# A 64-byte row instead of an 8-byte row in a routing table that is scattered to DRAM

## The chip, the cores and the metric

The kernel runs on one core of one Trainium2 chip. The metric is the device time of one execution in microseconds (us). The core has a matrix engine (PE, with its weight loads as PEld), a vector engine (DVE), a scalar engine (ACT), a general engine (POOL, GpSimd) and a queue engine (SP). DMAs are issued from SP and from POOL.

## The reference

The kernel computes block-causal attention and then a two-level mixture of experts on its output.

```
q, k, v: [8 batches, 8 heads, 576 positions, 64], float32
scores = q k^T / 8, masked so that block i (64 positions) sees blocks j <= i
x = softmax(scores) v, as 4608 tokens x 512
g      = argmax(x w_group)       over 4 groups, weight from the softmax
e      = argmax(x w_expert[g])   over 4 experts of the group, weight from the softmax
out[t] = (group weight * expert weight) * (relu(x[t] w1[g,e]) w2[g,e])
w1[g,e]: 512 x 1024, w2[g,e]: 1024 x 512, 16 experts in all
```

Each token is sent to one expert of 16. So between the two halves there is a routing step, which groups the tokens by expert.

## The kernel before, in words

**Attention.** Work goes by pairs of heads: 4 pairs in a batch, 32 pairs. One pass of the loop (a period) runs the tokens of a list that is written out by hand (`ORDER`): scores of one pair, row maxima, exponentials, transposes, the products with v, and the preparation of the next pair. The engines' queues keep the order of this list. In a plain period the products with v of one half head pair (`PE o L329`, 20 matmuls) come 11.3 us apart.

**The moves of q and k.** Each pair needs copies of its transposed q and k in the other half of the partitions. POOL makes them: `shift` (line 234, three moves a period, tokens W0 to W2), `dup` (lines 221 to 224) and `pad` (line 230). The score matmuls (`PE s L254`) read what these moves write, so PE waits if POOL is late.

**The router.** When the last pair of a batch is through, the tokens of the batch's router run among those of the next pairs: logits, argmax, and a rank of each token within its expert (`phase0` to `phase4`). Then `scatter` (line 802) writes one row for each token into a table in DRAM, `tab`: 16 experts with 5120 rows each and 640 rows behind them that stand for "no token", 82,560 rows in all. A row holds two 32-bit numbers, the token's number and its weight. The 576 rows of a batch go in five indirect DMAs from POOL, four of 128 rows and one of 64, each behind a tiny memset of `mark`. The rank makes tokens of one expert lie side by side in the table. In the hand-written list the five scatters (tokens Z0 to Z4) stand between the moves W0 and W1 of a period, and the program makes the first move behind them wait until all five have landed. For the first five batches that place is the same; in the sixth batch three scatters stand ahead of the move at line 221 and two between W0 and W1. The scatters of batches seven and eight have no moves of q and k behind them.

**The fill.** Before the first scatter the whole table is filled with "no token". `setup` does this from POOL in the periods 2 to 7 of attention, as a generator that hooks call five times a period.

**The readers.** In the second half, `getids` (line 881) reads an expert's part of the table back into SBUF with DMAs from SP, 37 in all. An indirect DMA from POOL then gathers the tokens' rows of x (line 892), PE transposes them and multiplies them with w1 and w2 (`h`, `y`), and another indirect DMA scatters the rows of the result, 2 KB each, to the output (line 1048). The weights stream in on SP's queue all the while.

Of the kernel before, what the change touches and what calls it, by code (L numbers as in the profile page):

```python
# [11 lines left out]
I32 = mybir.dt.int32  # L12
# [5 lines left out]
P = 128  # L18
# [393 lines left out]
NTB = 5  # L412
# [3 lines left out]
PADS = NE * REG  # L416
TABR = PADS + 640
R = 64
UNIT = 16
FULL = 512 // UNIT  # L420
CAPS = [33, 28, 28, 26, 20, 20, 18, 17, 16, 16, 12, 9, 9, 8]
# [12 lines left out]
class Router:  # L434
# [10 lines left out]
    def setup(self):  # L445
        nc, fixed = self.nc, self.fixed
        w = fixed.tile([P, 4, 64], F32, name="wcat")
        nc.vector.memset(w, 0.0)
        for z in range(2):
            ps, c0 = slice(64 * z, 64 * z + 64), 32 * z  # L450
            yield
            nc.gpsimd.dma_start(w[ps, :, c0:c0 + 4], self.w_group.rearrange("(c p) g -> p c g", p=P)[ps])
            for g in range(4):
                yield
                nc.gpsimd.dma_start(w[ps, :, c0 + 4 + 4 * g:c0 + 8 + 4 * g],
                                  self.w_expert[g].rearrange("(c p) e -> p c e", p=P)[ps])
        self.w = w
        self.lt = fixed.tile([P, 2, NTB * P], F32, name="lt")
        nc.vector.memset(self.lt[:, :, S:], 0.0)
        yield  # L460
        self.desc = fixed.tile([P, NTB, 4], F32, name="desc")
        for j in range(4):
            nc.gpsimd.memset(self.desc[:, :, j], float(4 - j))
        self.ones = fixed.tile([P, P], BF16, name="ones")
        nc.gpsimd.memset(self.ones, 1.0)
        self.tri = fixed.tile([P, P], BF16, name="tri")
        nc.gpsimd.affine_select(out=self.tri, in_=self.ones, pattern=[[1, P]], compare_op=ALU.is_gt,
                                fill=0.0, base=0, channel_multiplier=-1)

        def iota(name, sh, pattern, cm, base=0):  # L470
            t = fixed.tile(sh, F32, name=name)
            nc.gpsimd.iota(t, pattern=pattern, base=base, channel_multiplier=cm,
                           allow_small_or_imprecise_dtypes=True)
            return t

        self.base = iota("base", [P, NE], [[REG, NE]], 0)
        self.eb = iota("eb", [R, NE], [[REG, NE]], 0)
        self.pid = iota("pid", [R, 1], [[0, 1]], 1)
        self.p512 = iota("p512", [R, 1], [[0, 1]], 512)
        self.p128 = iota("p128", [R, 1], [[0, 1]], 128)  # L480
        self.edesc = iota("edesc", [R, NE], [[-1, NE]], 0, NE)
        yield
        self.vals = fixed.tile([R, 3, 2, NE], F32, name="vals")
        nc.gpsimd.iota(self.vals[:, 0], pattern=[[0, 2], [1, NE]], base=0, channel_multiplier=0,
                       allow_small_or_imprecise_dtypes=True)
        nc.gpsimd.memset(self.vals[:, 1], float(FULL))
        self.scan = [fixed.tile([R, 2 * NE], F32, name=f"scan{i}") for i in range(2)]
        for t in self.scan:
            nc.gpsimd.memset(t, 0.0)
        self.onesf = fixed.tile([R, R], F32, name="onesf")  # L490
        nc.gpsimd.memset(self.onesf, 1.0)
        self.trif = fixed.tile([R, 2, R], F32, name="trif")
        for z, op in ((0, ALU.is_ge), (1, ALU.is_gt)):
            nc.gpsimd.affine_select(out=self.trif[:, z, :], in_=self.onesf, pattern=[[1, R]], compare_op=op,
                                    fill=0.0, base=0, channel_multiplier=-1)
        self.pre = [fixed.tile([P, NTB + 1, NE], BF16, name=f"pre{i}") for i in range(2)]
        for t in self.pre:
            nc.vector.memset(t[:, 0, :], 0.0)
        self.mark = fixed.tile([1, 1], F32, name="mark")
        self.taken = fixed.tile([R, NE], F32, name="taken")  # L500
        yield
        fill = fixed.tile([P, 128, 2], I32, name="fill")
        nc.gpsimd.memset(fill[:, :, 0], NTOK)
        nc.gpsimd.memset(fill[:, :, 1], 0)
        for h in range(5):
            nc.gpsimd.dma_start(self.tab[h * 16384:(h + 1) * 16384].rearrange("(p c) t -> p c t", p=P), fill)
            yield
        nc.gpsimd.dma_start(self.tab[PADS:TABR].rearrange("(p c) t -> p c t", p=P), fill[:, 0:(TABR - PADS) // P, :])
        zrow = self.rows.tile([1, 512], F32, tag="row", name="zrow")
        nc.vector.memset(zrow, 0.0)  # L510
        nc.gpsimd.dma_start(self.xd[NTOK:NTOK + 1, :], zrow)
        yield
        self.cap = fixed.tile([R, 1], F32, name="cap")
        nc.gpsimd.memset(self.cap, 0.0)
        for n, c in enumerate(sorted(set(CAPS))):
            nc.gpsimd.affine_select(out=self.cap, in_=self.cap, pattern=[[0, 1]], compare_op=ALU.is_ge, fill=float(c),
                                    base=-sum(1 for x in CAPS if x >= c), channel_multiplier=1)
            if n % 4 == 3:
                yield
        yield  # L520
# [40 lines left out]
    def final(self, row):  # L561
# [4 lines left out]
        ri = self.t(dt=I32)  # L566
        stt(x, UNIT - 1.0, self.taken, ALU.add, ALU.subtract, out=ri)
        fi = ts(ri, 9, ALU.arith_shift_right, dt=I32)
        ci = ts(ri, UNIT.bit_length() - 1, ALU.arith_shift_right, FULL - 1, ALU.bitwise_and, dt=I32)
        cf, ff = self.t(), self.t()  # L570
# [45 lines left out]
    def spill(self, at, row, cnti):  # L616
# [5 lines left out]
        xi = self.t(one, I32)  # L622
        ts(x, 0.0, ALU.max, P // UNIT - 1.0, ALU.add, out=xi)
        xi = ts(xi, (P // UNIT).bit_length() - 1, ALU.arith_shift_right, sh=one, dt=I32)
        ov = self.t(one)
        V.tensor_copy(ov, xi)
        st = stt(self.cap, float(UNIT), self.res[:, 2:3], ALU.mult, ALU.add, sh=one)
        rhs = self.t([R, 4, R])
# [118 lines left out]
    def phase2(self, at, b, st):  # L747
        nc = self.nc
        full = [P, NTB, 4, 4]
        o16 = self.pool.tile(full, BF16, tag="o16", name=f"o16{b}")  # L750
        st["o16"] = o16
        nc.vector.tensor_tensor(
            out=o16, in0=st["goh"].unsqueeze(3).broadcast_to(full),
            in1=st["eoh"].unsqueeze(2).broadcast_to(full), op=ALU.mult)
        nc.vector.memset(o16[64:128, 4], 0.0)
        pre = self.pre[b % 2]
        for z in range(NTB):
            nc.vector.tensor_tensor(out=pre[:, z + 1, :], in0=pre[:, z, :],  # L758
                                    in1=o16[:, z].rearrange("p g e -> p (g e)"), op=ALU.add)
        gs = self.pool.tile([P, NTB], F32, tag="gs", name=f"gs{b}")  # L760
        es = self.pool.tile([P, NTB], F32, tag="es", name=f"es{b}")
        nc.vector.tensor_reduce(out=gs, in_=st["gex"], op=ALU.add, axis=AX.X)
        nc.vector.tensor_reduce(out=es, in_=st["eex"], op=ALU.add, axis=AX.X)
        nc.vector.tensor_scalar_add(es, es, 1e-9)
        nc.vector.scalar_tensor_tensor(out=gs, in0=gs, scalar=1e-9, in1=es, op0=ALU.add, op1=ALU.mult)
        pay = self.pool.tile([P, NTB, 2], I32, tag="pay", name=f"pay{b}")
        st["pay"] = pay
        nc.gpsimd.iota(pay[:, :, 0], pattern=[[P, NTB]], base=b * S, channel_multiplier=1)
        nc.vector.reciprocal(pay[:, :, 1].bitcast(F32), gs)
# [56 lines left out]
class Moe:  # L826
# [41 lines left out]
    def getids(self, s):  # L868
        if "ids" in s:
            return  # L870
        self.index(s)
        nc = self.nc
        s["ids"] = ids = self.ip.tile([P, 5, 2], I32, tag="ids", name=f"ids{s['n']}")
        table = lambda o, n: self.ro.tab[bass.ds(s["st"] + o, n), :]
        full = s["T"] // P
        todo = [(ids[:, 0:full, :], table(0, full * P).rearrange("(c p) t -> p c t", p=P))] if full else []
        r = s["T"] % P
        if r:
            todo += [(ids[z:z + r, full, :], table(full * P, r)) for z in ((0, s["gap"]) if s["tail"] else (0,))]
        for o, i in todo:  # L880
            self.ro.after_writes(nc.sync.dma_start(o, i))
# [313 lines left out]
def attention_moe(ctx, tc, q, k, v, w_group, w_expert, w1, w2, out, order=None, on_dve=None):  # L1195
    nc = tc.nc
# [2 lines left out]
    NBAT = q.shape[0]  # L1199
    N = 4 * NBAT  # L1200
    dp = ctx.enter_context(tc.tile_pool(name="dp", bufs=1, space=bass.MemoryType.DRAM))
    tab = dp.tile([TABR, 2], I32, name="tab")
    xd = dp.tile([NTOK + 1, 512], F32, name="xd")
    cp = ctx.enter_context(tc.tile_pool(name="cp", bufs=1))
    consts = make_consts(tc, cp)
# [6 lines left out]
    with tc.manual_schedule(engines={ET.PE, ET.Activation, ET.DVE, ET.Pool, ET.SP}):  # L1212
# [34 lines left out]
        b = lambda kk, j: ro.token(at, last, (kk, j))  # L1247
# [62 lines left out]
```

## Time and profile before

| what | value |
|---|---|
| time, median of 3 runs | 932.01 us (930.56 to 936.88) |
| the profiled execution's own time | 927.65 us |
| its span in the profile | 925.9 us |
| busy share of the span: PE, PEld, DVE, ACT, POOL | 93%, 78%, 63%, 56%, 37% |
| mean granted clock of PE | 0.972 |
| attention, up to about | 445 us |
| scatters to the table (line 802) | 40, 994 ns each on POOL, 6.0 us in the middle from issue to landing |
| fills of the table (line 506) | 5 of 128 KB, 2.1 us in the middle from issue to landing |

The profile is of one execution; the times of the runs differ from it by up to 9 us. A line such as `PE s L254 <- POOL qk L234: 31.2, 6, 8.3` in the view of waits says that PE at line 254, which writes `s`, waited for what POOL wrote to `qk` at line 234, for 31.2 us in total, six times, at most 8.3 us. In the view in order of time a row gives the start, the duration, the engine, the line, what is written and read, the count, and in brackets the idle time before it with what ended it. In the chain of waits a DMA's row runs from its issue to its landing. A granted clock of 1.00 is PE's full speed.

### The profile page before, as it was taken

The page shows a single profiled execution, that of the slowest core. Times are in us where ns is not written, and L with a number is a line of the kernel's source. Part 1 is how long each engine was busy: PE and PEld are TensorE (multiplying, and loading weights), DVE is VectorE, ACT ScalarE, POOL GpSimd, SP SyncE. Part 2 cuts the span into 40 slices and gives each one's busy share as a digit, 9 for nine tenths or more (in the row PEclk, how much of TensorE's full clock was granted, in tenths as well). Part 3 has the DMA queues.
Part 4 walks back from the last instruction along what each step waited for, and adds up shares of the span by engine and source line. Part 5 has one row for each costly group of instructions (what it writes and reads, how often), then busy time and mean ns, then how long its engine had stood idle before and what let it go on. Part 6 is the DMA issues. An engine that isn't in the chain of part 4 may idle for free.

```text
span 925.9 us, 16914 instructions
## 1 busy us (share of the span) xinstructions
PE 864.8 (93%) x5649; PEld 723.6 (78%) x5649; DVE 584.3 (63%) x1390; ACT 520.4 (56%) x1374; POOL 343.0 (37%) x555
## 2 busy tenths in 40 slices
PE   7999978989897998969998999999999999999996
PEld 5788857767785876757676887888888888988885
DVE  6778866878787796865873425446354465655562
ACT  6988866868786685856432425344243354645451
POOL 7785435454643545443251312322121123122011
PEclk9999998999999898998998999999999999999999
DMA  5452541526244252515732546555565557655671
GB/s 118 101 121 63 119 88 44 118 46 145 63 107 100 56 114 39 123 34 178 91 104 108 173 141 218 169 175 171 177 203 153 153 193 229 208 186 166 179 240 41
DMA packets 181432, 121.59 MB, mean 131 GB/s; under 512 B 125814, under 2 KB 156534, under 8 KB 181344
## 3 DMA queue, kind: packets, MB, share of 16 engines
q1 hardware_dynamic: 173296, 100.73, 41.4%
q0 software_dynamic: 8048, 19.76, 6.4%
q8 instruction: 46, 0.75, 0.4%
q14 instruction: 42, 0.34, 0.2%
HBM read 100.88 MB, written 19.70 MB: 130 GB/s over the span
## 4 chain that ended last, share of the span: by engine, by line
PE 72%; DVE 9%; DMA 8%; POOL 4%; issue 3%; ACT 3%; SPq 0%; POOLq 0%; DVEq 0%; ACTq 0%
PE h L977 17%; PE y L1022 17%; PE s L254 7%; PE o L329 7%; PE tp L297 6%; DMA tab<-pay,pi 5%; PE y L1027 4%; PE h L972 3%; DVE nm L268 2%; POOL tab L802 2%; PE tp L176 2%; PE ye L1022 2%; PE xp L945 2%; DVE pre L758 2%; DVE qk L200 2%
## 5 line engine op out<-in xcount | busy, mean ns | idle before, releaser
L268 DVE TENSOR_REDUCE nm<-s 128x1 f32<-128x384 f32 (+4 forms) x288 | 142.3, 513 | 81.2 <-PE s L254 79.3
L278 ACT ACTIVATE pb<-s,nm 128x384 f32<-128x384 f32 (+4 forms) x288 | 160.1, 562 | 38.0 <-DVE nm L268 37.2
L254 PE MATMUL s<-qk 128*128 128x256 f32 (+3 forms) x512 | 139.3, 365 | 42.4 <-POOL qk L234 31.2
L977 PE MATMUL h<-xt,wh 128*128 128x264 f32 (+6 forms) x704 | 155.3, 312 | 0.0
L929 DVE TENSOR_TENSOR wl<-raw,wh 128x512 fp32r<-128x512 f32 x192 | 123.5, 684 | 10.6 <-ACT wh L928 10.3
L977 PEld LDWEIGHTS h<-xt,wh 128*128 128x128 f32 x704 | 119.3, 188 | 9.1
L309 ACT COPY pt<-tp 128x512 f32<-128x512 f32 (+1 forms) x224 | 116.9, 548 | 13.8 <-PE tp L297 13.1
L254 PEld LDWEIGHTS s<-qk 128*128 128x128 f32 x512 | 78.5, 197 | 58.8 <-POOL qk L234 32.6
L234 POOL CAST qk<-qk 64x1152 fp32r<-64x1152 f32 x93 | 107.2, 1153 | 34.9 <-DMA tab<-pay,pi 31.9
L297 PE MATMUL tp<-ident,pb 128*128 128x128 f32 x800 | 114.8, 279 | 0.5 <-ACT pt L309 0.4
L1048 POOL DMA_INDIRECT out_dram<-ys,ids x40 | 42.5, 1062 | 187.1 <-DVE ys L1044 175.2
L977 PE MATMUL h<-xt,wl 128*128 128x264 f32 (+6 forms) x352 | 109.3, 311 | 0.0
L928 ACT CAST wh<-raw 128x512 fp32r<-128x512 f32 x192 | 109.1, 620 | 0.2
L1022 PE MATMUL y<-wh,hring 128*128 128x512 f32 x306 | 107.2, 401 | 0.0
L994 DVE SCALAR_TENSOR_TENSOR hring<-h,hring 128x32 fp32r<-128x32 f32 (+7 forms) x112 | 35.7, 356 | 103.1 <-ACT hring L990 99.9
L329 PE MATMUL o<-pt,vb 128*64 128x320 f32 (+4 forms) x896 | 100.5, 364 | 0.1
L297 PEld LDWEIGHTS tp<-ident,pb 128*128 128x128 f32 x800 | 95.1, 144 | 4.9 <-issue 1.2
L990 ACT ACTIVATE hring<-h 128x288 fp32r<-128x288 f32 (+7 forms) x62 | 28.9, 466 | 118.7 <-PE h L977 53.7
L329 PEld LDWEIGHTS o<-pt,vb 128*64 128x64 f32 x896 | 60.1, 137 | 41.2 <-issue 6.4
L892 POOL DMA_INDIRECT xg<-xd,ids x40 | 40.4, 1011 | 104.5 <-DMA ids<-tab 46.5
L221 POOL CAST qk<-qk 64x576 fp32r<-64x576 f32 x31 | 20.6, 665 | 139.5 <-DVE qk L307 121.4
L977 PEld LDWEIGHTS h<-xt,wl 128*128 128x128 f32 x352 | 66.2, 188 | 1.2
(228 smaller groups left out, 1512.3 us busy)
## 6 DMA issues: line engine op xcount, KB each, us to landing
raw<-in_moe_w_dram SPq DMA_DIRECT2D x96, 512.0 KB, 4.1
natk<-in_k_dram SPq DMA_DIRECT2D x32, 256.0 KB, 3.7
natq<-in_q_dram SPq DMA_DIRECT2D x32, 256.0 KB, 4.4
vb<-in_v_dram SPq DMA_DIRECT2D x64, 128.0 KB, 3.1
xd<-xns SPq DMA_DIRECT2D x32, 256.0 KB, 2.6
wh<-in_moe_w_dram SPq DMA_DIRECT2D x16, 512.0 KB, 5.0
rawe<-in_moe_w_dram SPq DMA_DIRECT2D x8, 512.0 KB, 6.8
natk<-in_k_dram SPq DMA_DIRECT2D x32, 32.0 KB, 4.0
```

What stands on the lines that cost most here:

```text
L234: self.nc.gpsimd.tensor_copy(o, s.bitcast(F32))
L254: nc.tensor.matmul(st[:, 0, 0:w], lhsT=r[a][z][:, q0:q0 + P], rhs=r[c][z][:, 0:w], start=x == 0, stop=x == 1)
L268: self.nc.vector.tensor_reduce(out=r["nm"][:, t:t + 1], in_=r["s", t], op=ALU.max, axis=AX.X if t < 8 else AX.XY, negate=True)
L278: nc.scalar.activation(reg, r.pop(("s", t)), AF.Exp, bias=r["nm"][:, t:t + 1], accum_out=self.sms[b][:, pr, t % 2, t // 2:t // 2 + 1])
L297: nc.tensor.transpose(out=o, in_=pb[:, POFF[x] + j * P:POFF[x] + (j + 1) * P], identity=self.c["ident"])
L309: self.nc.scalar.copy(dst, src)
L329: nc.tensor.matmul(o[64 * a:64 * a + 64, BLK * (t - b0):n], lhsT=r["v"][:, a, j, :], rhs=p[:, a], start=x == 0, stop=x == len(pcs) - 1, ti ...
L928: nc.scalar.copy(h[:, sl], s["raw", u][:, sl])
L929: nc.vector.tensor_tensor(out=l[:, sl], in0=s["raw", u][:, sl], in1=h[:, sl].bitcast(F32), op=ALU.subtract)
L977: nc.tensor.matmul(o, lhsT=ww[:, dc, f], rhs=rr[:, dc, t], start=dc == 0 and x == 0, stop=dc == 3 and x == 2)
L1022: nc.tensor.matmul(y[c][0:n], lhsT=hh, rhs=w, start=k == 0 and x == 0, stop=k == 7 and x == 2)
L1048: i = nc.gpsimd.indirect_dma_start(out=self.out, out_offset=bass.IndirectOffsetOnAxis(ap=s["ids"][0:n, c, 0:1], axis=0), in_=ys[0:n], in_o ...
```

## The change

A row of the table becomes 16 numbers of 32 bits (64 bytes), of which the first two are used as before. The table grows from 0.66 to 5.28 MB. Four things follow:

- The fill is a tile of 64 rows of 64 bytes on each partition (4 KB), cleared whole and then given its first column. It goes out in ten DMAs of 512 KB where there were five of 128 KB, two for each call of the generator.
- The payload of the scatter (`pay`) has 16 numbers for each token. It lies in two fixed tiles, which are cleared once beside the fill and used in turn, where it had two buffers of a pool.
- The scatter writes 64 bytes for each token. Its code is the same.
- The readers take the first two numbers of each row, so they still move 8 bytes for each token, now 64 bytes apart.

```diff
+TROW = 16
@@ setup
-        fill = fixed.tile([P, 128, 2], I32, name="fill")
+        fill = fixed.tile([P, 64, TROW], I32, name="fill")
+        nc.gpsimd.memset(fill, 0)
         nc.gpsimd.memset(fill[:, :, 0], NTOK)
-        nc.gpsimd.memset(fill[:, :, 1], 0)
-        for h in range(5):
-            nc.gpsimd.dma_start(self.tab[h * 16384:(h + 1) * 16384].rearrange("(p c) t -> p c t", p=P), fill)
-            yield
+        self.pays = [fixed.tile([P, NTB, TROW], I32, name=f"pay{i}") for i in range(2)]
+        for t in self.pays:
+            nc.gpsimd.memset(t, 0)
+        for h in range(10):
+            nc.gpsimd.dma_start(self.tab[h * 8192:(h + 1) * 8192].rearrange("(p c) t -> p c t", p=P), fill)
+            if h % 2:
+                yield
@@ phase2
-        pay = self.pool.tile([P, NTB, 2], I32, tag="pay", name=f"pay{b}")
+        pay = self.pays[b % 2]
@@ getids
-        table = lambda o, n: self.ro.tab[bass.ds(s["st"] + o, n), :]
+        table = lambda o, n: self.ro.tab[bass.ds(s["st"] + o, n), 0:2]
@@ attention_moe
-    tab = dp.tile([TABR, 2], I32, name="tab")
+    tab = dp.tile([TABR, TROW], I32, name="tab")
```

The order of the instructions is the same on PE, DVE, ACT and SP. It differs on POOL, at the fill. POOL's queue there, before:

```order
L503 MEMSET fill 128x128
L504 MEMSET fill 128x128
L506 DMA tab<-fill 128x256
L230 CAST qk_123<-qk_123 64x576
L223 CAST qk_123<-qk_123 64x512
L224 CAST qk_123<-qk_123 64x64
L506 DMA tab<-fill 128x256 x2
L221 CAST qk_122<-qk_122 64x576
L234 CAST qk_122<-qk_122 64x1152
L506 DMA tab<-fill 128x256 x2
L234 CAST qk_122<-qk_122 64x1152 x2
```

And POOL's queue at the same place in the changed kernel, whose lines behind the fill are numbered up to five higher:

```order
L504 MEMSET fill 128x1024
L505 MEMSET fill 128x64
L508 MEMSET pay_901 128x80
L508 MEMSET pay_902 128x80
L510 DMA tab<-fill 128x1024 x2
L230 CAST qk_123<-qk_123 64x576
L223 CAST qk_123<-qk_123 64x512
L224 CAST qk_123<-qk_123 64x64
L510 DMA tab<-fill 128x1024 x4
L221 CAST qk_122<-qk_122 64x576
L234 CAST qk_122<-qk_122 64x1152
L510 DMA tab<-fill 128x1024 x4
```

Two memsets and one DMA more stand ahead of the moves at lines 230 to 224, and two DMAs more at each of the two places that follow.

At the scatters the order stays. POOL's queue with the semaphores that it waits for, first group of scatters, before:

```order
L802 DMA tab<-pay_1761,pi_1831 82560x2
L801 MEMSET mark 1x1 [waits Pool_49]
L802 DMA tab<-pay_1761,pi_1831 82560x2
L801 MEMSET mark 1x1 [waits Pool_49]
L802 DMA tab<-pay_1761,pi_1831 82560x2
L234 CAST qk_123<-qk_123 64x1152 [waits DMASW3_49,DMASW4_49,DMASW2_49,DMASW5_49,DMASW1_49,DVE_49]
```

The same place in the changed kernel:

```order
L807 DMA tab<-pay_901,pi_1839 82560x16
L806 MEMSET mark 1x1 [waits Pool_49]
L807 DMA tab<-pay_901,pi_1839 82560x16
L806 MEMSET mark 1x1 [waits Pool_49]
L807 DMA tab<-pay_901,pi_1839 82560x16
L234 CAST qk_123<-qk_123 64x1152 [waits DMASW2_49,DMASW6_49,DMASW1_49,DMASW7_49,DMASW0_49,DVE_49]
```

The move at line 234 waits for five DMA semaphores (`DMASW`), one for each scatter, before and after; only their numbers moved, since five more DMAs of the fill took their turns.

## The prediction

> **What bounds the kernel now.** I read the page first, then the view of waits, the chain of waits in order of time, and PE in order of time at the places that these name. By the page PE is busy for 93% of the span, so a gain has to come from the places where PE stands still or runs slowly. Of PE's waits one is much longer than the others, and POOL's queue shows its cause:
>
> ```profile
> PE s L254 <- POOL qk L234: 31.2, 6, 8.3
> POOL qk L234 <- DMA tab<-pay,pi: 31.9, 6, 8.9
> ```
>
> PE's scores wait for POOL's moves of q and k, and those wait for the scatters to the table. The chain of waits has seven scatters in it (start, us from issue to landing), each the last that a move waits for:
>
> ```profile
> 130.40 9.71 DMA tab<-pay,pi
> ...
> 189.73 4.42 DMA tab<-pay,pi
> ...
> 242.54 3.96 DMA tab<-pay,pi
> ...
> 293.63 7.70 DMA tab<-pay,pi
> ...
> 350.68 5.78 DMA tab<-pay,pi
> ...
> 398.95 6.63 DMA tab<-pay,pi
> ...
> 409.24 4.99 DMA tab<-pay,pi
> ```
>
> PE in order of time shows six stalls, one for each of the first six batches (idle time in brackets):
>
> ```profile
> 141.46 1.22 PE L254 MATMUL s<-qk 128*128 128x512 f32 x2 [8.34 <-POOL qk L234]
> ```
> ```profile
> 195.64 1.22 PE L254 MATMUL s<-qk 128*128 128x512 f32 x2 [3.06 <-POOL qk L234]
> ```
> ```profile
> 247.84 0.74 PE L254 MATMUL s<-qk 128*128 128x512 f32 x2 [2.48 <-POOL qk L234]
> ```
> ```profile
> 302.67 1.22 PE L254 MATMUL s<-qk 128*128 128x512 f32 x2 [6.18 <-POOL qk L234]
> ```
> ```profile
> 357.86 1.22 PE L254 MATMUL s<-qk 128*128 128x512 f32 x2 [4.34 <-POOL qk L234]
> ```
> ```profile
> 415.57 1.22 PE L254 MATMUL s<-qk 128*128 128x512 f32 x2 [6.77 <-POOL qk L234]
> ```
>
> They add up to 31.17 us. In the first five, landing less stall is 1.37, 1.36, 1.48, 1.52 and 1.44 us: a stall is the landing of the last scatter less about 1.4 us, one for one. In the sixth two landings (6.63 and 4.99) stand ahead of one stall. There is a second price. The same two matmuls take 0.74 us behind the shortest stall and 1.22 behind the others. About 4 us behind each stall, with the granted clock as the first number behind the five engines' busy times:
>
> ```profile
> 141.46:145.50 4.04, 4.04 (x16) 3.65 (x17) 1.92 (x5) 2.17 (x7) 2.54 (x4) 0.50 0.02 4
> 195.64:199.70 4.06, 4.06 (x21) 3.67 (x22) 2.17 (x5) 2.21 (x8) 2.54 (x4) 0.64 0.00 0
> 247.84:251.90 4.06, 4.05 (x30) 3.79 (x31) 3.25 (x8) 3.12 (x10) 3.68 (x6) 1.00 0.01 1
> 302.67:306.70 4.03, 4.03 (x16) 3.63 (x17) 1.90 (x5) 2.17 (x7) 2.54 (x4) 0.50 0.00 0
> 357.86:361.90 4.04, 4.04 (x16) 3.65 (x17) 1.92 (x5) 2.17 (x7) 2.54 (x4) 0.50 0.01 2
> 415.57:419.60 4.03, 4.03 (x16) 3.64 (x17) 1.25 (x2) 1.83 (x5) 3.67 (x6) 0.50 0.74 197
> ```
>
> Behind the stall of 2.48 us the clock is full; behind 3.06 it is 0.64, and behind the longer ones 0.50 for 4 us. So a stall of 3 us and more costs another 1.5 to 2 us: length times (1 - clock) gives 2.0 four times and 1.5 once, 9.5 us. A stall of up to 2.5 us costs itself alone. The Trainium skill, "TensorE: Matmul & The Clock Gate", Part 1, says that an idle window of about 3.4 us halves PE's clock until it has been busy that long again; the rows agree, with the step somewhere between 2.48 and 3.06 us here.
>
> **The change, part by part.**
>
> *The scatter writes 64 bytes for a token.* POOL's instruction has the same 128 indices, and I cost it the same, since rows of 2 KB (line 1048) and of 8 bytes (line 802) take nearly the same time to issue:
>
> ```profile
> L1048 POOL DMA_INDIRECT out_dram<-ys,ids x40 | 42.5, 1062 | 187.1 <-DVE ys L1044 175.2
> ```
> ```profile
> L802 POOL DMA_INDIRECT tab<-pay,pi x40 | 39.8, 994 | 28.0 <-DVE pi L796 19.0 <-issue 8.0 <-POOL mark L801 1.0
> ```
>
> The question is the landing. While the fourth group is under way, from 298.7 us to its landing at 301.3 us, the bus is empty:
>
> ```profile
> DMA packets 2, 0.00 MB, mean 0 GB/s; under 512 B 2, under 2 KB 2, under 8 KB 2
> ```
>
> The data are out, and only the word that they have landed is late. So bandwidth isn't what holds the scatter. The nearest operation is the scatter of the result: same queue, same kind of instruction, rows of 2 KB. In the stretch 850 to 921 us its landings are
>
> ```profile
> DMA to landing us min/median/max: 1.9/2.8/4.0
> ```
>
> and in its group of 557 to 564 us, where weights and other transfers are on the bus,
>
> ```profile
> DMA to landing us min/median/max: 4.5/6.0/7.8
> ```
>
> That bounds a 64-byte scatter by 1.9 and 7.8 us; below 1.9 nothing is in sight, since POOL's instruction alone takes 1 us of it. The fourth group, the second longest, had a quiet bus at its end, so I stay near the quiet rows: 3.4 us, the middle between 2.8 (whole rows of 2 KB, quiet) and 4.0 (3.96, the best of the seven with 8-byte rows). Why should it fall at all? Tokens of one expert lie side by side, so eight 8-byte rows share 64 bytes, and 128 writes of one scatter meet in a few such places. That the landing of a DMA of whole rows is short and that of 8-byte rows long with an empty bus is what I would expect if those writes are put through one after another. It is an inference; no row shows it.
>
> With 3.4 us a stall is 2.0 us: five stalls make 10.0, and the sixth 6.77 - (6.63 - 3.4) - (4.99 - 3.4) = 1.95. That removes 31.17 - 11.95 = 19.2 us. All stalls are then under 2.48, so the 9.5 us of slow clock go too. Behind them PE itself is next, which is busy nearly all of a plain period.
>
> *The fill.* The prices of POOL's instructions on the page:
>
> ```profile
> L891 POOL MEMSET xge<- 128x512 f32 x4 | 2.1, 535 | 0.0
> L506 POOL DMA_DIRECT2D tab<-fill x5 | 2.8, 557 | 0.3 <-POOL fill L504 0.3
> ```
>
> and the place in POOL's time:
>
> ```profile
> 59.57 0.23 POOL L503 MEMSET fill<- 128x128 int32 x1
> ...
> 60.84 0.68 POOL L230 CAST qk<-qk 64x576 fp32r<-64x576 f32 x1
> 61.45 0.62 POOL L223 CAST qk<-qk 64x512 fp32r<-64x512 f32 x1
> ```
>
> From the first memset to the move at 230 it is 1.27 us now. After: a memset of 1024 columns, 2 x 0.535 = 1.07; three small ones at 0.23 each, the row at 59.57 (estimate); the 0.3 of wait that stands on the page; two issues, 1.11. That is 3.17 us, 1.9 more. Here PE waits for these moves already:
>
> ```profile
> PEld s L254 <- POOL qk L223: 0.5, 2, 0.3
> ```
>
> So the 1.9 us go through to PE. The other four issues (4 x 0.557 = 2.2 us) and what is carried along fall ahead of moves that PE needs later:
>
> ```profile
> 66.32 2.35 POOL L234 CAST qk<-qk 64x1152 fp32r<-64x1152 f32 x2
> ```
> ```profile
> 71.74 0.73 PE L254 MATMUL s<-qk 128*128 128x512 f32 x2
> ```
>
> The move ends at 68.7 and PE needs it at 71.7, later by its own delay of 1.9: 4.9 us of cover against 4.1, so nothing. Without that cover it would be at most 2.2 us.
>
> *The bytes of the fill.* 5.24 MB on the bus between 60 and about 80 us, beside loads of q, k and v of 0.86 MB a period. Large writes run at
>
> ```profile
> DMA packets 220, 0.39 MB, mean 279 GB/s; under 512 B 29, under 2 KB 29, under 8 KB 220
> ```
>
> (stores of x, 297.2 to 298.6 us). (5.24 + 0.86) / 0.279 = 21.9 us, so all is through at 82 us. The load that is needed first is that of v:
>
> ```profile
> 67.15 0.60 SPq L157 DMA_DIRECT2D vb<-in_v_dram  x1
> ```
> ```profile
> 84.02 0.87 PE L329 MATMUL o<-pt,vb 128*64 128x256 f32 x8
> ```
>
> It is needed at 84.0 + 1.9 = 85.9. Hidden, with 4 us to spare. At the mean of 62.8 to 67 us,
>
> ```profile
> DMA packets 2315, 0.90 MB, mean 214 GB/s; under 512 B 2231, under 2 KB 2231, under 8 KB 2314
> ```
>
> it would end at 88.5 (28.5 us) and cost 2.6 us; that is my upper bound. The first scatter waits for the fill, but only at 125 us.
>
> *The readers* move as many pieces of 8 bytes, from places 64 bytes apart. Their DMAs make POOL wait, and PE waits for the gather behind them once:
>
> ```profile
> POOL xg L892 <- DMA ids<-tab: 46.5, 6, 15.1
> ...
> PE xp L945 <- DMA xg<-xd,ids: 4.3, 1, 4.3
> ```
>
> I take nothing, and 1 us at most if the first load lands later. The two fixed payload tiles take turns as the two buffers did: nothing.
>
> **The sum.** 19.2 + 9.5 - 1.9 = 26.8 us off the profiled execution's own 927.65 us: 900.9. The median of the runs, 932.01, lies 4.4 us above; the same 26.8 off it is 905.2. Landings differ from 3.96 to 9.71 within one execution, and if that luck makes the spread of the runs, it goes with it. I forecast **903 us**. With a landing of 2.8 the stalls are 1.4 (five) and 0.75, 7.75 in all: 23.4 + 9.5 - 1.9 = 31.0, 896.6.
>
> **Rivals.**
>
> *Only the long ones shrink.* The landing falls to 4.2 us, between 3.96 and 4.42, as the two quickest groups have it with 8 bytes. Stalls: 5 x 2.8 and 3.55, 17.6 in all, 13.6 less; of the 9.5 us of clock half, since 2.8 lies between 2.48 and 3.06. 13.6 + 4.8 - 1.9 = 16.5: 911 to 915 us. For it: 3.96 and 4.42 come close to the 2 KB rows' 2.8 to 4.0. Against it: nothing names a cause that would spare them.
>
> *A write of 64 bytes is as slow as one of 8.* What a small write costs isn't the neighbours but that it is small, and 64 bytes are small. The landings stay, and the fill remains: 927.65 + 1.9 = 929.5, by the median 933.9. This is also the case in which the change does nothing of what it does. For it: no row of this trace has a write to DRAM between 8 bytes and 2 KB, apart from the fill's 1 KB, which lands in 2.1 us by the table above. Against it: nothing separates the two readings. The Trainium skill, "DMA: Bandwidth & Descriptors", Specifications, says that below 512 bytes a DMA engine reads, changes and writes back; by that rule 64 bytes would gain nothing over 8.
>
> *Slower: landing goes by the number of places.* If eight neighbours are taken together now, a scatter touches some 16 to 32 places of 64 bytes and then 128. Landings would go to the 2 KB rows' worst, 7.8 us, against a mean of 6.17 now (43.19 / 7). (7.8 - 6.17) x 7 = 11.4 us of stalls, 2.5 of clock (the groups at 2.48 and 3.06 go to half clock for 4 us), 1.9 of fill: 15.8, 943.5 us, by the median 947.8. It decides from a mean landing of about 7 us. Against it: 2 KB rows touch most places and land soonest when the bus is quiet.
>
> **Chances.** Forecast 0.44, the weaker gain 0.22, nothing 0.22, slower 0.12. The range reaches from the landing of 2.8 us (896.6, less a little for the spread: 895) to the case of nothing by the median (934); the slower case is left out. A change of 1% is about what a measurement of this kernel can tell from none, so faster is below 922.7 us: 0.66. Within 1% is the case of nothing: 0.22. Slower: 0.12.
>
> **What would show it.** The wait of the score matmuls for POOL falls from 31.2 to about 12 us; the seven landings are about 3.4; no stretch behind a group has the clock at 0.50; PE loses about 2 us near 64 us to the moves behind the fill. If the landings stay at 4 to 10 us, the inference on 8-byte rows is wrong. If they fall and the time doesn't, something behind PE in the same period was as late, and I have missed it. If PE waits for `vb` or `natk` between 80 and 95 us, the fill's bytes weren't hidden.

## The result, and the profile after

| what | before | after |
|---|---|---|
| time, median (lowest to highest), 4 runs each | 931.28 us (923.77 to 936.88) | 899.12 us (897.42 to 901.33) |
| span of the profiled execution | 925.9 us | 895.7 us |
| mean granted clock of PE | 0.972 | 0.994 |

The ratio is 0.966, with a 95% interval of 0.959 to 0.973. The forecast was 903 us, its range 895 to 934. One run of a later experiment (E7) took 1196.51 us at a granted clock of 0.654 and is left out of its figures.

The view of waits of the changed kernel (us in all, times, longest). PE has no row for POOL's moves at line 234 any more; its longest rows are these:

```profile
PE s L254 <- ACT pb L278: 11.4, 17, 1.3
PE xp L950 <- DMA xg<-xd,ids: 5.0, 1, 5.0
PE xn L678 <- ACT xT L309: 4.9, 5, 1.4
PE o L329 <- ACT lt L309: 2.0, 5, 0.4
```

And of POOL's rows those on the table:

```profile
POOL xg L897 <- DMA ids<-tab: 44.8, 6, 14.3
...
POOL qk L234 <- DMA tab<-pay,pi: 6.6, 5, 1.4
...
POOL qk L221 <- DMA tab<-pay,pi: 2.0, 1, 2.0
```

POOL's wait for the scatters at line 234 went from 31.9 us to 6.6 and PE's wait for POOL there from 31.2 to nothing. The first group of scatters in order of time, with the last scatter at 130.25 us:

```profile
127.54 2.22 PE L329 MATMUL o<-pt,vb 128*64 128x320 f32 x20
...
130.25 0.97 POOL L807 DMA_INDIRECT tab<-pay,pi  x1 [0.22 <-issue]
...
132.61 0.43 ACT L309 COPY xT<-o 128x320 f32<-128x320 f32 x1 [3.14 <-PE xn L678]
132.67 2.35 POOL L234 CAST qk<-qk 64x1152 fp32r<-64x1152 f32 x2 [1.45 <-DMA tab<-pay,pi]
132.72 0.62 DVE L268 TENSOR_REDUCE nm<-s 128x1 f32<-128x256 f32 x2 [3.07 <-PE xn L678]
...
133.09 0.66 PE L678 MATMUL xn<-ident,xT 128*128 128x128 f32 x4 [1.39 <-ACT xT L309]
```

The move behind the last scatter starts 2.42 us after that scatter's start; before it was 9.86 us (130.40 to 140.26). Something else is late now. ACT's copy of `o` needs the 20 matmuls that end at 129.76 us, and starts only at 132.61; DVE is held up as long. Before, the same matmuls ended at 129.94 us and ACT's copy started at 129.99, with 0.34 us of idle time ahead of it. PE then waits for ACT, 1.39 us here. The same stands behind the last scatter of each of the first five batches.

Behind it the clock is full; the same 4 us as the prediction's first stretch, in the same columns:

```profile
134.94:139.00 4.06, 4.06 (x32) 3.80 (x31) 3.26 (x8) 3.74 (x13) 2.63 (x6) 1.00 0.34 127
```

The distance from one start of the 20 matmuls at line 329 to the next gives what a period with scatters takes. Its first one, before and after:

```profile
127.72 2.22 PE L329 MATMUL o<-pt,vb 128*64 128x320 f32 x20
...
151.42 2.27 PE L329 MATMUL o<-pt,vb 128*64 128x320 f32 x20
```
```profile
127.54 2.22 PE L329 MATMUL o<-pt,vb 128*64 128x320 f32 x20
...
142.07 2.28 PE L329 MATMUL o<-pt,vb 128*64 128x320 f32 x20
```

That is 23.70 us and 14.53 us. All periods with scatters, read in this way, in this and the later runs:

| kernel | six periods with scatters, us | sum |
|---|---|---|
| before | 23.70, 16.96, 15.00, 21.16, 19.04, 21.03 | 116.89 |
| after | 14.53, 14.19, 14.67, 14.29, 14.74, 13.52 | 85.94 |
| after, once more (E5) | 13.46, 13.12, 13.15, 13.22, 13.14, 13.78 | 79.87 |
| before, once more (E10) | 20.57, 15.45, 14.84, 19.00, 15.45, 20.78 | 106.09 |
| 64-byte rows, 8 bytes written (E1) | 13.40, 13.15, 13.14, 13.18, 13.12, 13.70 | 79.69 |
| the same, eight neighbours in 64 bytes (E11) | 21.56, 18.87, 16.12, 20.74, 18.76, 21.09 | 117.14 |
| the same, four neighbours in 64 bytes (E12) | 18.22, 13.11, 13.15, 16.03, 14.04, 15.22 | 89.77 |
| rows of 16 bytes (E3) | 14.77, 13.09, 13.13, 16.07, 13.96, 13.28 | 84.30 |
| rows of 32 bytes (E2) | 13.43, 13.13, 13.15, 13.19, 13.16, 13.32 | 79.38 |
| rows of 128 bytes (E8) | 13.42, 13.11, 13.16, 13.19, 13.14, 13.17 | 79.19 |
| 64-byte rows, scatters elsewhere (E4) | 12.46, 12.46, 12.46, 12.45, 12.46, 13.10 | 75.39 |

After against before, that is 30.95 us; the period ahead of the sixth is 0.97 us longer now (14.16 against 13.19), which leaves 29.98. The spans differ by 30.2 us. So the whole gain lies in these periods, and the half behind attention is as long as it was (484.6 us behind the last start of the 20 matmuls, 484.2 before).

The fill in the changed kernel, POOL in order of time:

```profile
59.63 0.96 POOL L504 MEMSET fill<- 128x1024 int32 x1
...
61.21 1.18 POOL L510 DMA_DIRECT2D tab<-fill  x2 [0.20 <-POOL pay L508]
62.38 0.68 POOL L230 CAST qk<-qk 64x576 fp32r<-64x576 f32 x1
```

The move at line 230 starts at 62.38 us, 1.5 later than before (60.84). PE's next round of 20 matmuls isn't later, before and after:

```profile
67.41 2.22 PE L329 MATMUL o<-pt,vb 128*64 128x320 f32 x20
```
```profile
67.50 2.22 PE L329 MATMUL o<-pt,vb 128*64 128x320 f32 x20
```

With the fill's bytes the share of the DMA engines goes from 0.51 to 0.86, but PE's busy time in the stretch stays, 22.93 of 23 us (stretch, length, busy PE, PEld, DVE, ACT, POOL with counts, clock, share of the DMA engines, GB/s), before and after:

```profile
57.00:80.00 23.00, 22.93 (x188) 18.59 (x186) 18.03 (x40) 19.58 (x61) 19.64 (x37) 1.00 0.51 119
```
```profile
57.00:80.00 23.00, 22.93 (x188) 18.61 (x186) 17.52 (x41) 19.80 (x62) 21.55 (x43) 1.00 0.86 287
```

### The profile page after: what moved, and what is told of

It is laid out like the page before. It is cut to its first block, busy times and chain, and to the rows that moved or that the text cites. A ratio compares the mean times of both kernels' runs of the same rounds, so it can differ in the third digit from the quotient of the medians.

```text
span 895.7 us, 16921 instructions
## 1 busy us (share of the span) xinstructions
PE 852.5 (95%) x5649; PEld 710.8 (79%) x5649; DVE 583.8 (65%) x1390; ACT 518.4 (58%) x1374; POOL 348.5 (39%) x562
## 4 chain that ended last, share of the span: by engine, by line
PE 80%; DVE 10%; ACT 4%; DMA 2%; issue 2%; SPq 0%; another core or an unknown queue 0%; POOLq 0%; DVEq 0%; ACTq 0%
PE y L1027 18%; PE h L982 17%; PE s L254 8%; PE o L329 8%; PE tp L297 7%; PE y L1032 4%; PE h L977 4%; DVE nm L268 3%; ACT pb L278 3%; PE tp L176 2%; PE xn L678 2%; PE s L263 2%; PE xp L950 2%; DVE pre L763 2%; DVE qk L200 2%; PE ye L1027 2%
## 5 line engine op out<-in xcount | busy, mean ns | idle before, releaser
L268 DVE TENSOR_REDUCE nm<-s 128x1 f32<-128x384 f32 (+4 forms) x288 | 141.9, 513 | 51.4 <-PE s L254 37.2
L254 PE MATMUL s<-qk 128*128 128x256 f32 (+3 forms) x512 | 134.2, 353 | 14.4 <-ACT pb L278 11.4
L934 DVE TENSOR_TENSOR wl<-raw,wh 128x512 fp32r<-128x512 f32 x192 | 123.5, 684 | 10.6 <-ACT wh L933 10.3
L297 PE MATMUL tp<-ident,pb 128*128 128x128 f32 x800 | 110.6, 273 | 0.5 <-ACT pt L309 0.4
L254 PEld LDWEIGHTS s<-qk 128*128 128x128 f32 x512 | 75.3, 190 | 30.9 <-ACT pb L278 15.4
L297 PEld LDWEIGHTS tp<-ident,pb 128*128 128x128 f32 x800 | 91.1, 140 | 4.3 <-ACT pt L309 0.6
L897 POOL DMA_INDIRECT xg<-xd,ids x40 | 42.1, 1054 | 101.5 <-DMA ids<-tab 44.8
```

Source lines behind the costliest of these rows:

```text
L254: nc.tensor.matmul(st[:, 0, 0:w], lhsT=r[a][z][:, q0:q0 + P], rhs=r[c][z][:, 0:w], start=x == 0, stop=x == 1)
L268: self.nc.vector.tensor_reduce(out=r["nm"][:, t:t + 1], in_=r["s", t], op=ALU.max, axis=AX.X if t < 8 else AX.XY, negate=True)
L297: nc.tensor.transpose(out=o, in_=pb[:, POFF[x] + j * P:POFF[x] + (j + 1) * P], identity=self.c["ident"])
L934: nc.vector.tensor_tensor(out=l[:, sl], in0=s["raw", u][:, sl], in1=h[:, sl].bitcast(F32), op=ALU.subtract)
```

## The experiments

Three questions were open. Why do 8-byte rows land late: because neighbours share 64 bytes, or because the writes are small? Where does the new idle time of ACT and DVE come from? And did the fill cost nothing because it is cheap, or because it is covered? E1 to E10 ran on one chip and E11 and E12 on another; which chip gave the two runs above isn't on record. Runs of the kernel before stood beside them: E1 to E4 with a median of 922.73 us for it, E5 to E10 with 924.74, E11 and E12 with one run of 924.24.

**E1: 64-byte rows, 8 bytes written.**

```diff
-        nc.vector.tensor_copy(pi, pf)
+        nc.vector.tensor_scalar(out=pi, in0=pf, scalar1=float(TROW // 2), scalar2=None, op0=ALU.mult)
...
-            out=self.tab, out_offset=bass.IndirectOffsetOnAxis(ap=st["pi"][0:n, c:c + 1], axis=0),
-            in_=st["pay"][0:n, c, :], in_offset=None)
+            out=self.tab.rearrange("n (z t) -> (n z) t", t=2), out_offset=bass.IndirectOffsetOnAxis(ap=st["pi"][0:n, c:c + 1], axis=0),
+            in_=st["pay"][0:n, c, 0:2], in_offset=None)
```

> The table keeps its 64-byte rows, with fill and readers as in the changed kernel, but a scatter writes only the first 8 bytes of a row: each index is 8 times the row. So the writes are as small as in the kernel before, and no two of them share 64 bytes. Theory A, of the prediction (8-byte neighbours that share 64 bytes are put through one after another): nothing changes against the changed kernel; the move behind the last scatter starts 2.2 to 2.4 us after that scatter's start, POOL's wait for the table at the first shift stays near 6.6 us, time 897 to 902 us. Theory B (a small write is slow because it is small): the move starts 4 to 10 us behind the last scatter, POOL's wait is near 32 us, PE's wait for these moves near 31 us, time 929 to 935 us.

Measured: 889.80 us (889.22 to 891.12), ratio 0.966 (0.960 to 0.973). In the chain of waits the last scatters of the groups land soon, though the writes have 8 bytes:

```profile
130.50 2.11 DMA tab<-pay,pi
...
179.54 2.11 DMA tab<-pay,pi
...
228.56 2.12 DMA tab<-pay,pi
```

The last scatter is the one that counts. An earlier one of a group can land later, 4.85 us behind its issue in the fourth group, and is still through first. PE's wait for the moves is there and small:

```profile
PE s L254 <- POOL qk L234: 3.4, 5, 0.9
```

**E11: the same, with eight neighbours in 64 bytes again.** One number differs from E1:

```diff
-        nc.vector.tensor_scalar(out=pi, in0=pf, scalar1=float(TROW // 2), scalar2=None, op0=ALU.mult)
+        nc.vector.tensor_scalar(out=pi, in0=pf, scalar1=1.0, scalar2=None, op0=ALU.mult)
```

> The kernel in which a scatter writes 8 bytes of each 64-byte row, with one number changed: the index is the row itself and no longer 8 times the row, so that eight neighbours share 64 bytes again. Table, fill, write size and order stay. The readers still read at the old places, so the second half works on wrong rows and few results are written; only attention is to be compared. Theory A (neighbours in 64 bytes wait for one another): the move behind the last scatter starts 3.8 to 8 us after it, as in the kernel before, instead of 2.25; PE's wait for POOL at the scores is 20 to 32 us instead of 3.4; periods with scatters of 14.8 to 21 us instead of 13.2. Theory H (the larger table or its fill made the landings short): 2.25 us and 13.2 us stay.

Measured: 928.08 us in one run, of which the half behind attention, on wrong rows, says nothing. The chain and PE's wait are as in the kernel before:

```profile
131.25 7.97 DMA tab<-pay,pi
...
188.46 5.56 DMA tab<-pay,pi
...
243.19 3.53 DMA tab<-pay,pi
```
```profile
PE s L254 <- POOL qk L234: 28.5, 6, 6.8
```

Table, fill and size of the writes are the same in E1 and E11, and only the places differ. Landings of 2.1 us became 3.5 to 8.0, and the six periods 79.69 became 117.14 us. The two ran on different chips, but E12, on E11's chip and with 2.0 for that number, takes 89.77. So it is how close the neighbours lie in the table, as theory A has it. Theories B and H have fallen. That the writes are put through one after another, A's mechanism, no row shows.

**E2, E3, E12: two and four neighbours.** E2 and E3 are the changed kernel with other row sizes:

```diff
-TROW = 16
+TROW = 8
```

> Rows of 32 bytes, written whole; two tokens of one expert that lie side by side share 64 bytes (eight did in the kernel before). Theory A: at most two writes in a row meet in one place, so the start of the move behind the last scatter is 2.3 to 3 us after it, time 898 to 903 us. Theory B with a bound at 64 bytes: as the kernel before, 4 to 10 us, 929 to 935 us. Theory B with a cost in steps of size: between the two, 3 to 5 us and 905 to 920 us.

```diff
-TROW = 16
+TROW = 4
```

> Rows of 16 bytes, written whole; four neighbours share 64 bytes. Theory A: a quarter to a half of the extra landing of the kernel before (mean 6.17 us against some 2.3): 3 to 4.5 us, PE's wait for the moves 5 to 18 us, time 903 to 918 us. Theory B with a bound at 64 bytes: 929 to 935 us.

E12 is E1 with `scalar1=2.0`:

> The same with the index twice the row: 8 bytes are written every 16 bytes, so four neighbours share 64 bytes and half of the bytes between them are not written. The readers read wrong places here too; only attention is to be compared. Theory A: as with rows of 16 bytes written whole, 2.2 to 3.8 us behind the last scatter, PE's wait for POOL 5 to 10 us, periods of 13.1 to 16 us. If what counts is the bytes that a scatter writes in one place rather than the number of its writes there (32 of 64 bytes as with two rows of 16): 2.25 us everywhere. If 8-byte writes are slow in themselves once any share 64 bytes: 4 us and more.

Measured: E2 891.05 us (889.30 to 891.74), ratio 0.968 (0.961 to 0.974). E3 896.54 us (895.95 to 897.04), ratio 0.973 (0.967 to 0.980). E12 900.83 us in one run. In E12, too, only attention is to be compared. PE's waits for the moves in E3 and in E12:

```profile
PE s L254 <- POOL qk L234: 7.5, 6, 2.3
```
```profile
PE s L254 <- POOL qk L234: 10.3, 6, 4.1
```

Two neighbours in 64 bytes cost nothing that can be seen: E2's periods are those of E1. Four cost in some batches: E3's periods of batches two and three stay at 13.1 us, the fourth is 16.07. Eight cost in all. So the loss begins between a distance of 32 bytes and one of 16. It goes by the distance and not by the bytes written: in E12 four writes put 32 bytes into 64 and cost, in E2 two put 64 there and don't. That 64 bytes is the size of the place that counts isn't shown. Places of 32 bytes, of which each takes one write without loss, fit these rows as well, and so does a loss that grows with how densely the writes lie. Why 8 bytes with gaps cost more than 16 whole bytes in the first and the sixth period (18.22 and 15.22 us against 14.77 and 13.28) stays open; E12 ran on another chip than E3.

**E4: the scatters in POOL's gap.** In the hand-written list Z0 to Z4 are taken from their places and put behind `P0` (only the line that takes them is shown):

```diff
-E3 P0 D1 G3:6 X1:5 X4:4 t4 E1 X2:4
+E3 P0  Z0:7 Z1:7 Z4:7 Z3:7 Z2:7 D1 G3:6 X1:5 X4:4 t4 E1 X2:4
```

> The changed kernel with the five scatters of a batch in another place of the hand-written list: behind the moves at line 224 of the same pass, where POOL has 5 to 7 us of idle time, instead of between the moves W0 and W1. In the changed kernel ACT (copy of o to xT) and DVE (maximum of s) sit idle for 2.1 to 3.3 us behind the last scatter of each of the first five batches, until about the time at which the move at line 234 starts. Theory C (that idle time belongs to the landing of the scatters): it goes from its old place, and a like stretch of 2 to 3 us stands behind the last scatter in its new place, about 8 us later; the time falls only if PE is ahead there, by 0 to 10 us: 889 to 900. Theory D (it belongs to the place in the program, or to POOL's wait in that place): it doesn't move with the scatters; PE's periods with scatters go from 14.3 to about 12.5 us, 887 to 891 us. Against both: the next pass's moves at lines 221 and 234 wait for the scatters and come 2 to 3 us later than in a plain period; if PE needs them sooner, a new wait for POOL of 1 to 3 us six times stands there and the time is 895 to 905 us.

Measured: 888.02 us (886.11 to 891.12), ratio 0.965 (0.958 to 0.971). The first five periods with scatters are 12.46 us, and none of the waits that were feared stands in the next passes. On theories C and D it says nothing, as E5 shows.

**E5: the changed kernel once more.**

> The changed kernel once more, nothing edited. With only 8 bytes of each 64-byte row written, or with 32-byte rows, a period with scatters took 13.1 to 13.4 us, and ACT and DVE had no idle time of 2 to 3 us behind the last scatter; the changed kernel's profile has 14.2 to 14.7 us and that idle time. Theory F (the whole 64-byte writes cause it): it is there again, 14.2 to 14.7 us a period, 896 to 901 us. Theory G (it belonged to that one execution or chip, not to the kernel): periods of 13.1 to 13.4 us, no such idle time, 888 to 892 us, the same as with 8 bytes written.

Measured: 890.03 us (888.99 to 893.03), ratio 0.963 (0.960 to 0.965). The idle time isn't there. ACT's copy starts right behind the matmuls, and the move of POOL comes as early as before:

```profile
129.86 0.43 ACT L309 COPY xT<-o 128x320 f32<-128x320 f32 x1 [0.34 <-PE o L329]
...
132.70 2.35 POOL L234 CAST qk<-qk 64x1152 fp32r<-64x1152 f32 x2 [1.44 <-DVE xns L685]
...
133.90 0.50 PE L254 MATMUL s<-qk 128*128 128x512 f32 x1 [0.91 <-POOL qk L234]
```

So theory G: it isn't a property of the kernel. It is hardly one of a single execution either, since all four runs of the first measurement took 897.4 us and more. What there, but not here, held ACT and DVE up for some 2 to 3 us behind the scatters stays open; the programs are the same. E1, E2 and E3 were forecast from the first measurement's periods, and came out 6.5 to 7.2 us below the ranges given for their times (E3 also because its landings, 2.1 to 3.5 us, were shorter than the 3 to 4.5 expected).

**E6: 32-byte rows, and the scatters in the gap.** E2's and E4's edits together.

> 32-byte rows and the scatters moved into POOL's gap behind line 224, both edits tried singly before (891.05 and 888.02 us). The periods with scatters should be 12.46 us as with 64-byte rows in that place, and the fill is half as long: 886 to 889 us. If two neighbours in 64 bytes cost something that the old place hid, the moves of the next pass come later and PE waits for POOL: 889 to 895.

Measured: 885.94 us (884.46 to 887.85), ratio 0.958 (0.955 to 0.961). The six periods sum to 75.26 us (12.46, 12.45, 12.46, 12.46, 12.47, 12.96), 4.6 less than E5's 79.87, and the medians differ by 4.1. This is the lowest median here, but only 2.1 us below E4's, and its periods are E4's within 0.2 us.

**E7 and E9: the scatters in the gap, 8-byte rows.** E4's edit, made to the kernel before.

> The kernel before with nothing but the scatters moved into POOL's gap behind line 224; rows stay at 8 bytes. The next pass's moves (lines 221 and 234) then wait for landings of 4 to 10 us instead of 2.3. Moved there, the 64-byte scatters cost PE nothing with 2.3 us. If POOL has 3 us or more to spare in the next pass: the stalls fall by 3 us each and more, 31.2 us to at most 15, and the clock loses less: 897 to 910 us. If it has none beyond 2.3 us: stalls as before, 918 to 925 us on this chip. If the landings shorten because nothing else of the period runs beside them: 890 to 897.

> The kernel before with the scatters moved behind line 224, once more, for a profile (its runs so far took 900.6 to 903.5 us). Behind the scatters the next pass's move at line 221 should start 4 to 8 us after the last of them, as the landings of 8-byte rows were in the old place, and PE should wait for POOL some 1 to 4 us six times, about 15 us with what the clock loses. If the landings are as short as 2.3 us here, the place made them long, and the 12 to 15 us between this and the 64-byte rows in the same place must lie elsewhere.

Measured: E7 900.56 to 903.54 us in four runs, ratio 0.976 (0.973 to 0.979); E9 902.79 us. E9's waits of POOL and PE (PE's longer ones are two, not the six that were expected):

```profile
POOL qk L221 <- DMA tab<-pay,pi: 18.9, 3, 8.3
...
PE s L254 <- POOL qk L234: 7.7, 2, 6.2
```

The landings are as long as in the old place: the next move starts 4.6 to 9.3 us behind the last scatter. Most of it lies in POOL's slack now. What is left: the periods behind the first five groups take 13.80, 12.05, 11.51, 13.01 and 12.43 us, 62.80 in all against 56.39 in E4, and the sixth group, where two scatters still stand between two moves, 20.65 against 13.10. That makes 14.0 us, and E9 is 14.8 above E4. So the place alone is worth some 22.5 us (924.74 less 902.2, the median of E7's four runs), two thirds of the 34.7 that the wider rows are worth on this chip (924.74 less E5's 890.03), and the two overlap.

**E8: rows of 128 bytes.** `TROW = 32`, so a fill of 10.6 MB.

> Rows of 128 bytes, written whole; the fill doubles to 10.6 MB. Theory F (whole writes of 64 bytes and more hold up ACT and DVE behind the last scatter, by their bytes): idle time of 3 to 5 us there, periods with scatters of 14.5 to 17 us. Theory G: 13.1 to 13.4 us as with 32 bytes. The fill should be through some 20 us later than with 64-byte rows (5.2 MB more at 279 GB/s), near 102 us, and the loads of q, k and v of that time come late: PE loses 0 to 10 us between 80 and 115 us.

Measured: 902.45 us in one run. The landings (2.11 us) and the periods with scatters stay as with 64 bytes. But the fill isn't covered any more. PE's waits in 78 to 105 us, POOL's wait that makes the move at line 223 late, and two stretches (columns as above):

```profile
PE o L329 <- DMA vb<-in_v_dram: 3.7, 1, 3.7
PE s L254 <- POOL qk L223: 3.5, 1, 3.5
```
```profile
POOL xd L516 <- DMA tab<-fill: 3.3, 1, 3.3
```
```profile
57.00:80.00 23.00, 18.76 (x152) 15.04 (x149) 13.38 (x29) 16.53 (x53) 18.30 (x32) 1.00 0.80 295
80.00:105.00 25.00, 21.32 (x146) 17.38 (x146) 16.60 (x35) 14.84 (x43) 12.61 (x23) 0.86 0.73 252
```

The two periods there take 17.17 and 17.98 us, in E5 11.82 and 12.45: 10.9 us lost, a little more than the 0 to 10 expected. So the 5.2 MB of the changed kernel cost nothing because they are through before anything that PE needs has to wait for them, and not because a fill is cheap. How much room is left no run shows.

**E10: the kernel before once more.**

> The kernel before once more, nothing edited, for a profile on the chip that ran the experiments, where its runs took 915 to 927 us against 924 to 937 before. If the seven landings are shorter here by about the difference, 1 to 1.5 us each (mean 4.5 to 5.5 us), the landings of 8-byte rows make the spread of its times. If they are as long as before (mean 6.2 us), the difference lies elsewhere: in the stretches in which ACT and DVE are held up, or behind attention.

Measured: 915.97 us in one run. The landings, of which four are shown:

```profile
130.81 7.76 DMA tab<-pay,pi
...
187.03 4.28 DMA tab<-pay,pi
...
238.37 3.77 DMA tab<-pay,pi
...
289.29 6.35 DMA tab<-pay,pi
```

All seven are 7.76, 4.28, 3.77, 6.35, 4.35, 5.72 and 6.30 us, 38.53 in all against 43.19, a mean of 5.5. The periods with scatters sum to 106.09 against 116.89 us, and the spans differ by 11.7 (914.2 against 925.9). So the landings and what hangs on them make up 10.8 of the 11.7 us between these two executions. But their order repeats: the first group is the longest and the third the shortest in the profile before, in E10 and in E11.

## Why the prediction was right, and where it wasn't

**The bound.** Right. The six stalls were the moves that wait for the scatters, and the whole gain lies in their periods.

**The stall is the landing less about 1.4 us.** Right, and it holds on the short side: in E5 and E1 the landing is 2.1 us, and a period with scatters takes 13.14 us where it takes 12.46 without the wait (E4), so the stall is 0.7. In the profile of the change itself no such stall is seen, since ACT was later there than the move.

**A landing of 3.4 us.** Too long: 2.1 us. I stood in the middle between the 2 KB rows' 2.8 and the best 8-byte group's 3.96. The lower end of the bound, 1.9, was the better guide. With 2.1 the prediction's own sum leaves stalls of 0.7 five times and none in the sixth: 31.17 - 3.5 = 27.7 us, with 9.5 of clock 37.2. The periods of E5 against those of the kernel before give 116.89 - 79.87 = 37.0. (Against E10, which ran on E5's chip, it is 26.2; that execution took 8.8 us less than the median there.) By the size of the landing the forecast was 8.5 us short (37.2 - 28.7).

**Why it falls.** Inferred then, shown now in its first half: E1 against E11 changes only how far apart neighbours are written, and E12 confirms it on E11's chip. The second half, that writes in one place go one after another, and that 64 bytes are such a place, is still an inference. By the reference's routing of its inputs, the 128 tokens of a scatter go to one to four experts, so that with 8-byte rows its writes meet in 16 to 18 places of 64 bytes. The rival that 64 bytes are as slow as 8 has fallen: the last scatters land in 2.1 us with 8 bytes alone in a place (E1), with 32 (E2), 64 (E5) and 128 (E8). The Trainium skill, "DMA: Bandwidth & Descriptors", Specifications, says that below 512 bytes a DMA engine reads, changes and writes back. No run here shows whether it does; the size of the write alone, which that rule goes by, doesn't set the landing here. The weaker gain (4.2 us) and the slower case (landing by the number of places) fell too; E1's scatters touch 128 places of 64 bytes and land as soon as any.

**The clock, 9.5 us.** All stretches behind the groups have the full clock, so the term is right for this kernel. The rule that it was built on, that a stall of up to 2.5 us costs itself alone, is wrong as a rule: that the stall of 2.48 us cost no clock was the luck of when it fell. Nor did the rows quite agree with an idle window of 3.4 us, as was said, since 3.06 us was enough. See the last section.

**The fill at PE, 1.9 us.** Wrong: 0.1 us. The moves at lines 230 to 224 were 1.5 us late and PE wasn't. The step that failed is "Here PE waits for these moves already". Its row, 0.5 us in two waits for line 223, was a sum over the span. In order of time the two stand at 49.89 and 71.74 us: one ahead of the fill, the other of 0.17 us some 9 us behind these moves. I took them for waits at 62 us without looking where they are. The second isn't even a wait for POOL: the changed kernel has the same 0.17 us at the same matmuls (71.83 us), although the next such moves end only at 74.66 there, 2.8 us later than before.

**The fill's bytes.** Hidden, as forecast, and by the cover named: E8 doubles them, and PE waits for v and for moves behind the fill. **The readers**: POOL waits 44.8 us for `ids` against 46.5; nothing, as taken.

**What I didn't see.** Nothing in the prediction has ACT and DVE late behind the scatters. In the profiled execution that took back most of what the shorter landing gave: its periods sum to 85.94 us, E5's to 79.87, 6.1 us, and 1.0 more in the period ahead of the sixth. The account: 26.8 forecast, 8.5 more from the landing, 1.8 more from the fill, 7.0 less from this, is 30.1 us; the spans differ by 30.2. So 899 came close to 903 partly by luck, with two errors against one another. In the runs of E5, where it doesn't happen, the changed kernel gains 34.7 us against the medians there (924.74 - 890.03).

I also took the differences between landings for luck within one execution. In part they aren't: which groups are longest and shortest repeats from run to run, while the first group's landing alone moved between 7.76 and 9.71 us. Why one group lands later than another stays open; by the routing, every scatter of 128 rows meets in 16 to 18 places.

## What to carry to other kernels

When a scatter of short rows is awaited, look at how close together its rows lie: the last scatter of a group landed in 2.1 us here with rows 32 bytes apart or more, in 3.5 to 9.7 with rows 8 bytes apart, and spacing the rows helped without writing more bytes. Then look at what stands behind the scatter in its queue: moving it to where its engine is idle gave some 22.5 us without any change of the rows. A row in the view of waits sums over the span; before its wait is charged with a delay, find in order of time where it stands.

## What the runs showed of the hardware that was not expected

**The granted clock after a short stall.** The length of the stall doesn't decide alone. Two stalls in E3 and one in E10:

```profile
136.26 0.73 PE L254 MATMUL s<-qk 128*128 128x512 f32 x2 [2.26 <-POOL qk L234]
...
284.71 1.15 PE L254 MATMUL s<-qk 128*128 128x512 f32 x2 [1.93 <-POOL qk L234]
```
```profile
192.81 0.73 PE L254 MATMUL s<-qk 128*128 128x512 f32 x2 [2.92 <-POOL qk L234]
```

The clock steps on a grid: within each profile here but E7's, the changes of the granted clock lie multiples of 3.413 us apart. So each window of this grid can be looked at by itself: its length and PE's busy time, and the clock as the third number from the end. First E3 with the window in which most of its stall of 2.26 us lies and the one after it, then with the stall of 1.93 us; then E10 with its stall of 2.92 us, and last the kernel before with its stall of 2.48 us.

```profile
134.63:138.04 3.41, 1.78 (x12) 1.61 (x13) 1.02 (x4) 0.86 (x4) 2.86 (x3) 1.00 0.33 123
138.04:141.45 3.41, 3.41 (x30) 3.32 (x29) 3.38 (x7) 3.18 (x10) 3.06 (x6) 1.00 0.02 5
281.40:284.81 3.41, 1.48 (x15) 0.92 (x13) 1.30 (x3) 1.34 (x6) 1.23 (x2) 1.00 0.42 154
284.81:288.23 3.42, 3.42 (x14) 3.03 (x15) 1.55 (x4) 1.74 (x6) 2.45 (x4) 0.50 0.00 0
```
```profile
191.19:194.60 3.41, 1.79 (x12) 1.62 (x13) 1.03 (x4) 0.86 (x4) 2.87 (x3) 1.00 0.23 47
194.60:198.02 3.42, 3.42 (x30) 3.33 (x29) 3.38 (x7) 3.20 (x10) 3.07 (x6) 1.00 0.00 0
```
```profile
242.97:246.38 3.41, 2.40 (x23) 1.84 (x21) 2.00 (x4) 2.36 (x9) 0.54 (x1) 1.00 0.20 72
246.38:249.79 3.41, 1.95 (x14) 1.77 (x15) 1.17 (x4) 1.01 (x4) 3.02 (x4) 1.00 0.46 86
```

The stall of 1.93 us lies in one window, which is idle for 1.93 of 3.41 us, and the next has half the clock. The stalls of 2.26, 2.92 and 2.48 us reach over two windows each, of which none is idle for more than 1.63 us, and the clock stays full. It is so throughout these profiles, from 40 us on: a window at full clock in which PE was idle for up to 1.63 us was followed by the full clock, and one in which it was idle for 1.97 us or more by half of it; between the two both occur. The Trainium skill, "TensorE: Matmul & The Clock Gate", Part 1, says that the gate watches a window of about 3.4 us that runs freely, so that it matters where in the window an event falls. With that these rows agree. The same part of the Trainium skill asks for a whole idle window ahead of the slow clock; here about half a window of idle time was enough.

**Signals behind the scatters.** In the first measurement of the changed kernel, ACT and DVE started 2 to 3 us after the matmuls that they need had ended, in five batches, and in E5's runs the same program didn't do so (0.34 us). No run here shows why, nor whether it went with the chip.
